# Logits, exponentials and slot products of the last pair in pieces, and row sums ahead of the second expert layer

## The chip, the cores and the metric

The kernel runs on one core of one Trainium2 chip. The metric is the device time of one execution in microseconds, as the median of several runs of a kernel.

## What is computed

Attention over keys and values that are averaged in groups of eight, and behind it a soft mixture of experts:

```python
k_p = k.reshape(B, H, Sp, pool, D).mean(axis=3)        # B = H = 8, S = 576, D = 64, pool = 8, Sp = 72
v_p = v.reshape(B, H, Sp, pool, D).mean(axis=3)
attn = softmax(scale * q @ k_p.T)
x = (attn @ v_p).transpose(0, 2, 1, 3).reshape(4608, 512)
logits = x @ phi                                       # 32 slots: 8 experts x 4
slot_input = softmax(logits, axis=0).T @ x             # over the 4608 tokens
slot_out[e] = relu(slot_input[e] @ w1[e]) @ w2[e]      # w1: 512 x 1024, w2: 1024 x 512, for each expert
out = softmax(logits, axis=1) @ slot_out
```

## The kernel before

The batch is worked off in four pairs of batch elements. A pair's tokens stand in nine tiles of 128 (t = 0 to 8), its heads in two halves of four (qd = 0, 1). For each half, eight score units (`score_unit`: two matmuls into `sc`, one ScalarE exponential into `exa`) are interleaved with nine `u_tile`s. A `u_tile` multiplies `exa` by the pooled values into a PSUM tile `u_ps` (two buffers), takes the reciprocal of the softmax sum on VectorE (`rec`), and scales the tile into `xsa`, on VectorE in one instruction or, with `by_scalar`, on ScalarE in four. The pooled values carry 32 more columns per head, the values' share of the slot logits. So each row of `xsa` holds per head 64 output values and 32 logit shares; summed over the heads these are the logits.

`dispatch` turns a pair into its share of the slot input. It sums the logit shares over the heads (`lg`), takes one exponential for all nine tiles (`ee`, ScalarE), and adds nine slot products `ee.T @ x` in `G_ps` on TensorE. For the first three pairs the sum over heads is eight matmuls with the identity, spread into the next pair's work by `combine`. For the last pair, with `by_vector`, it is one VectorE reduction over all nine tiles. `add_up` adds the result to the other pairs' (`Gb` for the last).

Then, in program order: `Gb` is transposed (`si_ps`), `turn` transposes `ee` into `cT` (the unnormalized weights of the last softmax), `hidden` makes the experts' first layer (`h_ps`, four experts side by side in TensorE's columns), `turn_hidden` transposes it (`hT_ps`). `hz` and `z_ps` prepare a correction for the last 128-row block of the last expert. `second_layer` adds the second layer in `so_ps`, experts 0 to 3, then 4 and 5, then 6 and 7 in pieces. `row_sums` sums `cT` over the slots with one-hot weights (`R_ps`), copies the sums to SBUF on ScalarE, transposes them (`RT_ps`) and takes their reciprocals. `busy(512)` is a dummy product of fp32 operands into `idle_ps`. At the end `begin` and `tiles` multiply tokens by slot outputs, scale them on ScalarE and VectorE in turn, and store them.

Up to the hidden layer a scheduler sets the order of TensorE, ScalarE and VectorE from the program; GpSimd keeps the written order throughout, and all engines do from `hidden` on. GpSimd issues all weight loads: w1 into `w1_sb` (named `w_sb` in the profile), w2 of experts 0 to 3 into the `big` buffers, 4 and 5 into `qTa`, 6 and 7 into `xsa`, the last in eight pieces by halves of the columns (L492), which wait until the slot products have read what they overwrite.

Of the kernel before, what the change touches and what calls it, by code (L numbers as in the profile page):

```python
# [18 lines left out]
def kernel(  # L19
# [66 lines left out]

    CUT6 = FJ - 5
    HC = DM // 2  # L90
    halves = [slice(0, HC), slice(HC, DM)]
    PIECES = ((E - 2, CUT6, FJ), (E - 1, 0, 4), (E - 1, 4, FJ - 1), (E - 1, FJ - 1, FJ))
# [215 lines left out]
        nc.scalar.activation(out=dst.rearrange("p r (i t) -> p r i t", t=NU),  # L308
                             in_=ps[:, :, 0:S // 2].rearrange("p r (t i) -> p r i t", i=NI), func=AF.Exp, scale=scale)

    def u_tile(pair, qd, t, ex, by_scalar=False):

        ps = ps_u.tile([128, HQ, XW + 1], FP, name="u_ps", tag="u")
        for hh in range(HQ):
            for b in range(2):
                if t < 8 and b != t // 4:
                    continue
                c = (t % 4 if t < 8 else 4) * 128
                rows = slice(0, 128) if t < 8 else slice(b * 64, (b + 1) * 64)
                nc.tensor.matmul(out=ps[rows, hh],  # L320
                                 lhsT=ex[b][:, hh].rearrange("p r t -> p (r t)")[:, c:c + rows.stop - rows.start],
                                 rhs=vp[(2 * pair + b) % 5][:, qd * HQ + hh, 0:XW + 1],
                                 start=True, stop=True)
        rec = small.tile([128, HQ], FP, name="rec", bufs=3)
        nc.vector.reciprocal(out=rec, in_=ps[:, :, XW])  # L325
        dst = xs[pair][:, t, qd * HQ:(qd + 1) * HQ, :]
        if by_scalar:
            for hh in range(HQ):
                nc.scalar.activation(out=dst[:, hh], in_=ps[:, hh, 0:XW], func=AF.Copy, scale=rec[:, hh:hh + 1])
        else:  # L330
            nc.vector.tensor_tensor(out=dst, in0=ps[:, :, 0:XW],  # L331
                                    in1=rec.rearrange("p h -> p h ()").to_broadcast([128, HQ, XW]), op=ALU.mult)

    def dispatch(x, ps, ee, by_vector=False):

        if by_vector:
            lg = small.tile([128, 9, NS], FP, name="lg", bufs=1)
            nc.vector.reduce_sum(out=lg, in_=x[:, :, :, D:XW].rearrange("p t h c -> p t c h"), axis=AX.X)  # L338
        else:
            lg = ps_m.tile([128, 9, NS], FP, name="lg_ps", tag="m")  # L340
            for h in range(H):
                nc.tensor.matmul(out=lg, lhsT=ident, rhs=x[:, :, h, D:XW], start=(h == 0), stop=(h == H - 1))
        nc.scalar.activation(out=ee, in_=lg.rearrange("p t s -> p t () s").to_broadcast([128, 9, NG, NS]), func=AF.Exp)  # L343
        yield
        for t in range(9):
            nc.tensor.matmul(out=ps, lhsT=ee[:, t].rearrange("p g s -> p (g s)"), rhs=x[:, t, :, 0:D],  # L346
                             start=(t == 0), stop=(t == 8))

# [22 lines left out]
    def combine(pair):  # L371

        ps = ps_m.tile([128, DM], FP, name="G_ps", tag="m")
        ee = small.tile([128, 9, NG, NS], BF, name="ee", bufs=1)
        parts = dispatch(xs[pair], ps, ee)
        next(parts)
        yield
        next(parts, None)
        add_up(pair, ps, G)
        yield  # L380
        for b in range(2):
            turn(pair, b, ee)
            yield
# [15 lines left out]
    for c, (n, t) in enumerate(quads + rest):  # L399
        for i in range(2 * t.shape[1]):  # L400
            place[n + i] = (i, c)

    def row_sums():

        ps = ps_m.tile([NC, 4, 128], FP, name="R_ps", tag="m")
        for c, (_, t) in enumerate(quads + rest):
            nc.tensor.matmul(out=ps[:, 0:2 * t.shape[1]].rearrange("p (s r) i -> p s r i", r=2),   # L407
                             lhsT=onehot[:, MAXC - 1 - c:MAXC - 1 - c + NC], rhs=t,
                             start=(c == 0), stop=(c == NC - 1), skip_group_check=True)
        sums = consts.tile([NC, 4, 128], FP)  # L410
        nc.scalar.copy(out=sums, in_=ps)
        ps = ps_m.tile([128, 4, NC], FP, name="RT_ps", tag="m")
        for i in range(4):
            nc.tensor.transpose(out=ps[:, i], in_=sums[:, i], identity=identf[0:NC, 0:NC])
        nc.vector.reciprocal(out=recR[:, 0:2], in_=ps[:, 0:2])
        nc.vector.reciprocal(out=recR[:, 2:4, 0:len(quads)], in_=ps[:, 2:4, 0:len(quads)])
# [21 lines left out]
    for pair in range(NP):  # L438
        for qd in range(2):
            if qd == 0:  # L440
                prep = chain(prepare_kq(pair + 1), prepare_v(pair + 1)) if pair + 1 < NP else None
                if pair == 0:
                    prep = chain(prepare_v(0), prep)
            ex = [exa[0:SP, (2 * pair + qd) % 2, b] for b in range(2)]
            for i in range(9):
                if i < 8:
                    score_unit(pair, i // 4 * H + qd * HQ + i % 4, ex[i // 4][:, i % 4])
                if i < 5:
                    if last is not None:
                        u_tile(*last[:2], 4 + i, last[2])  # L450
                else:
                    u_tile(pair, qd, i - 5, ex)
                step(prep)
                if pair == 0 and i % 2:
                    step(prep)
                if qd == 0 and pair > 0:
                    if i == 4:
                        comb = combine(pair - 1)
                        step(comb)
                    if i == 7:  # L460
                        step(comb)
                if qd == 1 and i in (2, 6):
                    step(comb)
            if qd == 1:
                for _ in prep or ():
                    pass
            last = (pair, qd, ex)
    load_w2(qTa, 4, 2)
    load_w2(xsa[:, 0:1], E - 2, 1, 0, CUT6)

    u_tile(*last[:2], 4, last[2], by_scalar=True)
    G_ps = ps_m.tile([128, DM], FP, name="G_ps", tag="m")
    ee = small.tile([128, 9, NG, NS], BF, name="ee", bufs=1)
    for i in range(1, 5):
        u_tile(*last[:2], 4 + i, last[2], by_scalar=i % 2 == 0)
    for _ in dispatch(xs[NP - 1], G_ps, ee, True):
        pass
    add_up(NP - 1, G_ps, Gb)
    def half_home(e, half):
        if e == E - 1:  # L480
# [66 lines left out]
    hidden(1)  # L547
    turn_hidden(0)
    turn_hidden(1)
    nc.vector.reduce_sum(out=recC, in_=C, axis=AX.X)  # L550
    nc.vector.reciprocal(out=recC, in_=recC)

# [15 lines left out]
    def busy(n):  # L568
        nc.tensor.matmul(out=idle[:, 0:n], lhsT=cTf[:, 0:128], rhs=cTf[:, 0:n], start=True, stop=True)
# [7 lines left out]
    so_a = post.tile([128, DM], BF)  # L577
    so = post.tile([128, DM], BF)

    out_a = exf.rearrange("p (n c) -> p n c", c=DM)  # L580
    out_b = w1f.rearrange("p (n c) -> p n c", c=DM)
    n = 0
    places = []
    for rows, base in GROUPS:
        home = out_a[:, n:n + rows] if n + rows <= 6 else out_b[:, n - 6:n - 6 + rows]
        places.append((home, out[base:base + 128 * rows].rearrange("(p r) c -> p r c", r=rows)))
        n += rows

# [42 lines left out]

    for e in range(4):
        second_layer(e)
    row_sums()
    busy(512)
    for e in range(4, E - 2):
        second_layer(e)
# [55 lines left out]
```

## Time and profile before

| | |
|---|---|
| median of 3 runs | 175.68 us (175.49 to 175.91) |
| profiled execution | span 179.6 us, the only time given for it |
| busy, of that span | PE 129.9, DVE 97.1, ACT 88.3, POOL 19.9 us |
| DMA | 41.13 MB moved, HBM read 61.93 MB, written 9.44 MB |
| mean granted TensorE clock | 0.892 |

Times in the rows are microseconds from the start of the span. PE is TensorE's matmuls, PEld its weight loads, DVE VectorE, ACT ScalarE, POOL GpSimd, SP the queue that issues the stores. L338 is line 338 of the kernel. In a timeline or group row stand the output and input tiles, their sizes, the count, and in brackets the idle time before and what ended it. In the chain of waits a row is start, length, engine, tile, line and count. In a table of windows each engine has its busy time and, in brackets, its instructions; the last three columns are the granted clock (1.00 is full), the share of the 16 DMA engines and GB/s. A matmul is counted with its drain, so the last of a group is longer than its share; a few matmul records can be missing.

### The profile page before, as it was taken

The page shows a single profiled execution, that of the slowest core. Times are in us where ns is not written, and L with a number is a line of the kernel's source. Part 1 is how long each engine was busy: PE and PEld are TensorE (multiplying, and loading weights), DVE is VectorE, ACT ScalarE, POOL GpSimd, SP SyncE. Part 2 cuts the span into 40 slices and gives each one's busy share as a digit, 9 for nine tenths or more (in the row PEclk, how much of TensorE's full clock was granted, in tenths as well). Part 3 has the DMA queues.
Part 4 walks back from the last instruction along what each step waited for, and adds up shares of the span by engine and source line. Part 5 has one row for each costly group of instructions (what it writes and reads, how often), then busy time and mean ns, then how long its engine had stood idle before and what let it go on. Part 6 is the DMA issues. An engine that isn't in the chain of part 4 may idle for free.

```text
span 179.6 us, 2853 instructions
## 1 busy us (share of the span) xinstructions
PE 129.9 (72%) x1106; PEld 70.2 (39%) x1106; DVE 97.1 (54%) x258; ACT 88.3 (49%) x168; POOL 19.9 (11%) x37
## 2 busy tenths in 40 slices
PE   0006888999899999999998996512996988798000
PEld 0002463565555655556555543300443232333000
DVE  5403353387868588785888629764335000599200
ACT  3201238986887649876599726232012012799100
POOL 7000111052100040000100004000700300000000
PEclk9999999999999999999999669655559999999755
DMA  5999999999999999999999999999999990699995
GB/s 197 242 209 233 207 220 216 213 224 203 204 220 216 216 207 220 225 204 219 208 230 204 221 217 210 228 206 223 214 210 207 196 181 7 225 342 428 480 394 235
DMA packets 10780, 41.13 MB, mean 229 GB/s; under 512 B 768, under 2 KB 6656, under 8 KB 7184
## 3 DMA queue, kind: packets, MB, share of 16 engines
q0 software_dynamic: 7440, 30.48, 83.9%
q1 hardware_dynamic: 3328, 10.49, 15.0%
q8 instruction: 8, 0.13, 0.3%
q14 instruction: 4, 0.03, 0.0%
HBM read 61.93 MB, written 9.44 MB: 397 GB/s over the span
## 4 chain that ended last, share of the span: by engine, by line
PE 51%; ACT 17%; DVE 14%; DMA 6%; issue 3%; POOL 1%; DVEq 0%; ACTq 0%; POOLq 0%
PE pool_ps L234 9%; ACT exa L308 7%; DMA phi_f<-in_moe_phi_dram 6%; PE G_ps L346 6%; PE sc L306 6%; PE u_ps L320 6%; PE q_ps L266 5%; DVE w_sb L575 4%; PE h_ps L521 3%; DVE xsa L331 3%; PE so_ps L542 3%; ACT vmeans L240 2%; DVE lg L338 2%; PE R_ps L407 2%; PE turn_ps L250 2%
## 5 line engine op out<-in xcount | busy, mean ns | idle before, releaser
L308 ACT ACTIVATE exa<-sc 72x576 bf16<-72x576 f32 x64 | 39.5, 652 | 5.1 <-PE sc L306 4.3
L331 DVE TENSOR_TENSOR xsa<-u_ps,rec 128x384 bf16<-128x384 f32 x69 | 37.4, 554 | 1.3
L320 PE MATMUL u_ps<-vp,exa 72*128 72x97 bf16 (+1 forms) x320 | 27.3, 217 | 4.5 <-DVE xsa L331 3.7
L320 PEld LDWEIGHTS <-exa 72*128 72x128 bf16 (+1 forms) x320 | 18.2, 104 | 16.0 <-DVE xsa L331 6.8
L306 PE MATMUL sc<-qTa,kp 64*72 64x288 bf16 x128 | 22.0, 309 | 1.9 <-ACT exa L308 1.5
L234 PE MATMUL pool_ps<-big,pmat 128*128 128x512 bf16 x64 | 18.6, 411 | 0.7 <-ACT qTa L270 0.6
L325 DVE RECIPROCAL rec<-u_ps 128x4 f32<-128x4 f32 x72 | 11.5, 172 | 12.8 <-PE u_ps L320 12.6
L346 PE MATMUL G_ps<-xsa,ee 128*128 128x512 bf16 x36 | 12.0, 496 | 6.6 <-ACT ee L343 6.6
L266 PE MATMUL q_ps<-ident,big 128*128 128x128 bf16 x144 | 12.5, 231 | 0.2
L186 PE MATMUL phi_ps<-spread,sel 128*128 128x256 bf16 x4 | 1.3, 397 | 15.1 <-DVE spread L181 15.1
L600 PE MATMUL f_ps<-so,cT 128*128 128x512 bf16 (+1 forms) x42 | 10.2, 337 | 1.8 <-ACT w_sb L573 0.8
L306 PEld LDWEIGHTS <-kp 64*72 64x72 bf16 x128 | 8.0, 108 | 8.3 <-issue 3.1
L575 DVE TENSOR_SCALAR w_sb<-f_ps,recR 128x512 f32<-128x512 f32 (+1 forms) x17 | 10.5, 683 | 0.4 <-PE f_ps L600 0.2
L266 PEld LDWEIGHTS <-big 128*128 128x128 bf16 x144 | 9.6, 104 | 2.4 <-issue 0.7
L242 DVE TENSOR_REDUCE rsum<-rest_ps 128x64 f32<-128x512 f32 x8 | 5.5, 692 | 9.3 <-PE rest_ps L238 9.2
L270 ACT COPY qTa<-q_ps 128x768 bf16<-128x768 bf16 x8 | 6.3, 794 | 7.8 <-PE q_ps L266 7.8
L272 DVE COPY qTa<-q_ps 128x768 bf16<-128x768 bf16 x16 | 8.8, 553 | 2.1 <-PE q_ps L266 2.0
L573 ACT ACTIVATE w_sb<-f_ps,recR 128x512 f32<-128x512 f32 (+1 forms) x17 | 9.6, 638 | 0.5 <-PE f_ps L600 0.3
L492 POOL DMA_DIRECT2D xsa<-in_moe_w_dram x8 | 6.0, 754 | 26.2 <-PE G_ps L346 15.3
L346 PEld LDWEIGHTS <-ee 128*128 128x128 bf16 x36 | 4.1, 120 | 12.3 <-ACT ee L343 6.8
L234 PEld LDWEIGHTS <-pmat 128*128 128x128 bf16 x64 | 5.8, 103 | 6.4 <-issue 2.3
L240 ACT CAST vmeans<-pool_ps 128x1024 bf16<-128x1024 f32 x4 | 4.0, 1012 | 6.8 <-PE pool_ps L234 6.8
(104 smaller groups left out, 155.1 us busy)
## 6 DMA issues: line engine op xcount, KB each, us to landing
w_sb<-in_moe_w_dram POOLq DMA_DIRECT2D x2, 3072.0 KB, 37.2
big<-in_q_dram POOLq DMA_DIRECT2D x4, 1152.0 KB, 12.0
big<-in_v_dram POOLq DMA_DIRECT2D x4, 1152.0 KB, 15.8
big<-in_moe_w_dram POOLq DMA_DIRECT2D x1, 4096.0 KB, 40.0
big<-in_k_dram POOLq DMA_DIRECT2D x3, 1152.0 KB, 21.4
out_dram<-w_sb SPq DMA_DIRECT2D x1, 3072.0 KB, 10.8
qTa<-in_moe_w_dram POOLq DMA_DIRECT2D x1, 2048.0 KB, 30.4
out_dram<-w_sb SPq DMA_DIRECT2D x1, 2048.0 KB, 7.5
```

The lines of the kernel that those rows point to most:

```text
L234: nc.tensor.matmul(out=ps, lhsT=pmat, rhs=src[:, t:full * POOL:POOL, :], start=(t == 0), stop=(t == POOL - 1))
L266: nc.tensor.transpose(out=ps[:, t].rearrange("p n i -> p (n i)"), in_=q_sb[pair][:, tt:tt + 2, :].rearrange("p t d -> p (t d)"), identity= ...
L272: nc.vector.tensor_copy(out=dst, in_=ps)
L306: nc.tensor.matmul(out=ps[:, r, 0:S // 2], lhsT=kp[pair][rows, n], rhs=qT[pair][rows, n].rearrange("p t i -> p (t i)"), start=True, stop=True)
L308: nc.scalar.activation(out=dst.rearrange("p r (i t) -> p r i t", t=NU), in_=ps[:, :, 0:S // 2].rearrange("p r (t i) -> p r i t", i=NI), fu ...
L320: nc.tensor.matmul(out=ps[rows, hh], lhsT=ex[b][:, hh].rearrange("p r t -> p (r t)")[:, c:c + rows.stop - rows.start], rhs=vp[(2 * pair + ...
L325: nc.vector.reciprocal(out=rec, in_=ps[:, :, XW])
L331: nc.vector.tensor_tensor(out=dst, in0=ps[:, :, 0:XW], in1=rec.rearrange("p h -> p h ()").to_broadcast([128, HQ, XW]), op=ALU.mult)
L346: nc.tensor.matmul(out=ps, lhsT=ee[:, t].rearrange("p g s -> p (g s)"), rhs=x[:, t, :, 0:D], start=(t == 0), stop=(t == 8))
L573: nc.scalar.activation(out=dst, in_=src, func=AF.Copy, scale=by)
L575: nc.vector.tensor_scalar(out=dst, in0=src, scalar1=by, scalar2=None, op0=ALU.mult)
L600: nc.tensor.matmul(out=ps, lhsT=tokens(n), rhs=so[:, cols], start=True, stop=True)
```

## The change

`dispatch` is split into `weigh` (logits by eight matmuls with the identity, then the exponential, for a range of tiles) and `gather` (the slot products of a range). The other pairs call both for all nine tiles. The last pair calls them for tiles 0 to 3, 4 to 6 and 7 to 8 in turn, and has no VectorE reduction. Tiles 6, 7 and 8 of its second half get places in the two `sc` buffers. ScalarE scales tiles 1, 3, 5 and 7 of that half, where it had 4, 6 and 8. `row_sums` moves from behind the second layer of experts 0 to 3 to behind `turn_hidden`; its second part, the transposes and reciprocals, stays where it was, as `turn_sums`. Four `busy(512)` follow it, where one did. Two constants are written otherwise with the same value.

```diff
-    CUT6 = FJ - 5
+    CUT6 = 3
...
-    def u_tile(pair, qd, t, ex, by_scalar=False):
-        ps = ps_u.tile([128, HQ, XW + 1], FP, name="u_ps", tag="u")
+    def u_tile(pair, qd, t, ex, by_scalar=False, ps=None):
+        if ps is None:
+            ps = ps_u.tile([128, HQ, XW + 1], FP, name="u_ps", tag="u")
...
-    def dispatch(x, ps, ee, by_vector=False):
-        if by_vector:
-            lg = small.tile([128, 9, NS], FP, name="lg", bufs=1)
-            nc.vector.reduce_sum(out=lg, in_=x[:, :, :, D:XW].rearrange("p t h c -> p t c h"), axis=AX.X)
-        else:
-            lg = ps_m.tile([128, 9, NS], FP, name="lg_ps", tag="m")
-            for h in range(H):
-                nc.tensor.matmul(out=lg, lhsT=ident, rhs=x[:, :, h, D:XW], start=(h == 0), stop=(h == H - 1))
-        nc.scalar.activation(out=ee, in_=lg.rearrange("p t s -> p t () s").to_broadcast([128, 9, NG, NS]), func=AF.Exp)
-        yield
-        for t in range(9):
+    def weigh(x, ee, t0, t1):
+        lg = ps_m.tile([128, t1 - t0, NS], FP, name="lg_ps", tag="m")
+        for h in range(H):
+            nc.tensor.matmul(out=lg, lhsT=ident, rhs=x[:, t0:t1, h, D:XW], start=(h == 0), stop=(h == H - 1))
+        nc.scalar.activation(out=ee[:, t0:t1], in_=lg.rearrange("p t s -> p t () s").to_broadcast([128, t1 - t0, NG, NS]),
+                             func=AF.Exp)
+
+    def gather(x, ps, ee, t0, t1):
+        for t in range(t0, t1):
             nc.tensor.matmul(out=ps, lhsT=ee[:, t].rearrange("p g s -> p (g s)"), rhs=x[:, t, :, 0:D],
                              start=(t == 0), stop=(t == 8))
...
-                    u_tile(pair, qd, i - 5, ex)
+                    u_tile(pair, qd, i - 5, ex, by_scalar=pair == NP - 1 and qd == 1 and i in (6, 8))
...
-    u_tile(*last[:2], 4, last[2], by_scalar=True)
+    x = xs[NP - 1]
     G_ps = ps_m.tile([128, DM], FP, name="G_ps", tag="m")
     ee = small.tile([128, 9, NG, NS], BF, name="ee", bufs=1)
-    for i in range(1, 5):
-        u_tile(*last[:2], 4 + i, last[2], by_scalar=i % 2 == 0)
-    for _ in dispatch(xs[NP - 1], G_ps, ee, True):
-        pass
+    wide = [ps_sc.tile([128, 2, 512], FP, name="sc") for _ in range(2)]
+    spare = [wide[i // 2][:, i % 2, 0:HQ * (XW + 1)].rearrange("p (h c) -> p h c", h=HQ) for i in range(3)]
+    for i in range(5):
+        u_tile(*last[:2], 4 + i, last[2], by_scalar=i % 2 == 1, ps=spare[i - 2] if i >= 2 else None)
+        if i == 2:
+            weigh(x, ee, 0, 4)
+    gather(x, G_ps, ee, 0, 4)
+    weigh(x, ee, 4, 7)
+    gather(x, G_ps, ee, 4, 7)
+    weigh(x, ee, 7, 9)
+    gather(x, G_ps, ee, 7, 9)
     add_up(NP - 1, G_ps, Gb)
...
     turn_hidden(1)
+    row_sums()
...
+    IN_A = 6
...
     for e in range(4):
         second_layer(e)
-    row_sums()
+    turn_sums()
+    busy(512)
+    busy(512)
+    busy(512)
     busy(512)
```

ScalarE before, from the last score exponential to the copies behind the hidden layer. `xsa` rows are quarter tiles, `ee` the exponential of the logits:

```order
L308 ACTIVATE exa<-sc 72x576
L329 ACTIVATE xsa<-u_ps,rec 128x96 x12
L343 ACTIVATE ee<-lg 128x1152
L526 ACTIVATE h_sb_1719<-h_ps 128x512
L526 ACTIVATE h_sb_1720<-h_ps 128x512
L562 CAST zT<-z_ps 128x256
L411 COPY sums<-R_ps 10x512
```

The same place now; `xsa<-sc` is a tile that was multiplied into one of the two `sc` buffers:

```order
L308 ACTIVATE exa<-sc 72x576
L330 ACTIVATE xsa<-u_ps,rec 128x96 x8
L340 ACTIVATE ee<-lg_ps 128x512
L330 ACTIVATE xsa<-u_ps,rec 128x96 x4
L330 ACTIVATE xsa<-sc,rec 128x96 x4
L340 ACTIVATE ee<-lg_ps 128x384
L340 ACTIVATE ee<-lg_ps 128x256
L536 ACTIVATE h_sb_1749<-h_ps 128x512
L536 ACTIVATE h_sb_1750<-h_ps 128x512
L411 COPY sums<-R_ps 10x512
L573 CAST zT<-z_ps 128x256
```

Three tiles by ScalarE have become four, the first exponential stands between the second and the third of them, and the copy of the row sums now stands ahead of `zT`.

TensorE before, behind the last `u_tile`:

```order
L320 MATMUL u_ps<-vp_103,exa 64x97
L346 LDWEIGHTS ee
L346 MATMUL G_ps<-xsa,ee 128x512
...
L361 LDWEIGHTS ee
L361 MATMUL c_ps<-ident,ee 128x128
```

and now, from the last logit matmul of the first piece (`sc` is tile 7):

```order
L339 MATMUL lg_ps<-xsa,ident 128x128
L346 LDWEIGHTS ee
L346 MATMUL G_ps<-xsa,ee 128x512
...
L321 MATMUL sc<-vp_103,exa 128x97
...
L346 MATMUL G_ps<-xsa,ee 128x512
L339 LDWEIGHTS ident
L339 MATMUL lg_ps<-xsa,ident 128x96
...
L339 MATMUL lg_ps<-xsa,ident 128x64
L346 LDWEIGHTS ee
L346 MATMUL G_ps<-xsa,ee 128x512
L361 LDWEIGHTS ee
L361 MATMUL c_ps<-ident,ee 128x128
```

The nine slot products stood together; now two stand ahead of tile 7, two behind it, three behind the second piece's logits and two behind the third's.

TensorE before, between the hidden layer's transposes and the second layer:

```order
L533 MATMUL hT_ps<-ident,h_sb_1720 128x128
L560 LDWEIGHTS hz
L560 MATMUL z_ps<-cT,hz 128x256
L542 LDWEIGHTS hT
L542 MATMUL so_ps<-big,hT 32x512
```

and now:

```order
L543 MATMUL hT_ps<-ident,h_sb_1750 128x128
L408 LDWEIGHTS onehot
L408 MATMUL R_ps<-cT,onehot 10x512
...
L408 MATMUL R_ps<-cT,onehot 10x256
L571 LDWEIGHTS hz
L571 MATMUL z_ps<-cT,hz 128x256
L552 LDWEIGHTS hT
L552 MATMUL so_ps<-big,hT 32x512
```

The ten products of `R_ps` stand ahead of `z_ps`; behind the second layer of experts 0 to 3 only the transposes `RT_ps` are left, with four dummy products after them.

More of the change, by code (lines that the diff above doesn't have):

```diff
@@ L374, in combine @@
         ee = small.tile([128, 9, NG, NS], BF, name="ee", bufs=1)
-        parts = dispatch(xs[pair], ps, ee)
-        next(parts)
+        weigh(xs[pair], ee, 0, 9)
         yield
-        next(parts, None)
+        gather(xs[pair], ps, ee, 0, 9)
         add_up(pair, ps, G)
@@ L401 @@
             place[n + i] = (i, c)
+    sums = consts.tile([NC, 4, 128], FP)
     def row_sums():
@@ L409, in row_sums, with turn_sums @@
                              start=(c == 0), stop=(c == NC - 1), skip_group_check=True)
-        sums = consts.tile([NC, 4, 128], FP)
         nc.scalar.copy(out=sums, in_=ps)
+    def turn_sums():
         ps = ps_m.tile([128, 4, NC], FP, name="RT_ps", tag="m")
@@ L584 @@
     for rows, base in GROUPS:
-        home = out_a[:, n:n + rows] if n + rows <= 6 else out_b[:, n - 6:n - 6 + rows]
+        home = out_a[:, n:n + rows] if n + rows <= IN_A else out_b[:, n - IN_A:n - IN_A + rows]
         places.append((home, out[base:base + 128 * rows].rearrange("(p r) c -> p r c", r=rows)))
```

## The prediction

> **What bounds the kernel now.** I read the windows of 1 us first, to see whether the memory or the engines set the end.
>
> ```profile
> 147.00:148.00 1.00, 1.00 (x17) 0.42 (x10) 0.00 (x0) 0.00 (x0) 0.00 (x0) 1.00 1.11 147
> 148.00:149.00 1.00, 1.00 (x5) 0.10 (x3) 0.00 (x0) 0.00 (x0) 0.00 (x0) 1.00 0.33 44
> 149.00:150.00 1.00, 1.00 (x11) 0.41 (x8) 0.00 (x0) 0.00 (x0) 0.00 (x0) 1.00 0.00 0
> ...
> 153.00:154.00 1.00, 0.86 (x13) 0.46 (x12) 0.96 (x3) 0.86 (x3) 0.00 (x0) 1.00 0.60 199
> ```
>
> The last three columns are the granted clock, the DMA share and GB/s. The loads run dry between 148 and 149 us, and the first result is stored from 153: for four microseconds memory waits for the engines. So the serial chain up to the first store sets the end; stores and final scaling follow it as a block. The chain that ended last, from the last token tiles to the second layer (start, length, what):
>
> ```profile
> 60.79 1.95 PE G_ps L346 x9
> ...
> 114.59 1.04 ACT xsa L329 x4
> ...
> 119.29 4.00 DVE lg L338
> 123.31 1.17 ACT ee L343
> 124.53 4.03 PE G_ps L346 x9
> 128.59 0.69 DVE Gb L353
> ...
> 130.33 5.32 PE h_ps L521 x58
> ...
> 136.33 0.73 PE hT_ps L533 x8
> ...
> 138.14 0.34 DVE hz L557
> 138.53 0.28 PE z_ps L560
> 138.81 1.84 PE so_ps L542 x32
> 140.65 3.99 PE R_ps L407 x10
> 144.66 0.58 ACT sums L411
> 145.29 0.41 PE RT_ps L414 x4
> 145.70 1.05 PE idle_ps L569 x2
> 146.76 0.98 PE so_ps L542 x16
> ...
> 151.07 0.48 ACT so_a L573
> ...
> 153.84 0.43 PE so_ps L542 x9
> ```
>
> Three steps (logits 4.00, exponentials 1.17, slot products 4.03 us) run strictly one after the other from 119.29 to 128.59. TensorE also idles 1.47 us from 137.06 (the end of hT_ps) to z_ps, and 0.65 us from the end of R_ps to RT_ps. The first row is the same slot product for another pair: 1.95 us, half of 4.03. The clock explains that:
>
> ```profile
> 99.00:100.00 1.00, 0.61 (x9) 0.43 (x6) 0.93 (x4) 0.81 (x2) 0.00 (x0) 0.83 0.98 205
> 106.00:107.00 1.00, 1.00 (x9) 0.49 (x8) 0.04 (x1) 0.00 (x0) 0.00 (x0) 0.76 1.25 262
> 113.00:114.00 1.00, 0.57 (x7) 0.38 (x8) 0.93 (x5) 0.00 (x0) 0.00 (x0) 0.66 0.74 156
> 133.00:134.00 1.00, 1.00 (x20) 0.39 (x12) 0.00 (x0) 0.03 (x1) 0.00 (x0) 0.60 0.78 164
> ```
>
> A granted clock between 0.50 and 1.00 dates the flip inside its row: down at 99.66, up at 106.48, down at 113.32, up at 133.80. Everything between 113.3 and 133.8, the stage that is edited, runs at half clock.
>
> **The change: the last tiles and the slot sums.** The last nine tiles (0 to 8 of the pair's second half) feed the logits. Prices:
>
> ```profile
> 109.95 0.65 ACT L308 ACTIVATE exa<-sc 72x576 bf16<-72x576 f32 x1
> 110.42 0.37 PE L320 MATMUL u_ps<-vp,exa 72*64 72x97 bf16 x8 [0.47 <-DVE xsa L331]
> 111.86 0.56 DVE L331 TENSOR_TENSOR xsa<-u_ps,rec 128x384 bf16<-128x384 f32 x1
> 113.22 0.56 DVE L331 TENSOR_TENSOR xsa<-u_ps,rec 128x384 bf16<-128x384 f32 x1
> 115.68 0.81 PE L320 MATMUL u_ps<-vp,exa 72*128 72x97 bf16 x8 [0.65 <-ACT xsa L329]
> 100.27 1.14 PE L342 MATMUL lg_ps<-xsa,ident 128*128 128x288 bf16 x4
> 133.97 0.60 ACT L526 ACTIVATE h_sb<-h_ps 128x512 bf16<-128x512 f32 x1 [9.49 <-PE h_ps L521]
> ```
>
> VectorE needs 0.68 us a tile (two pitches from 111.86 to 113.22), of which some 0.12 are the reciprocal that it keeps for ScalarE's tiles too; ScalarE needs 1.04 us. ScalarE now takes tiles 1, 3, 5 and 7 (before 4, 6, 8). Three tiles have PSUM places of their own, so tiles 6 and 8 are multiplied early; their last weights come from the exponential that ends at 110.60, and they stand before tile 8 of the first half (110.42 before), which holds that one to about 110.75 and VectorE by some 0.2 us: tile 0 ends at 112.64 instead of 112.42.
>
> From there, with 0.05 us a hand-over and four products at half clock 0.45: ScalarE has tile 1 from 112.8 to 113.8 and tile 3 from 114.6 to 115.65 (its PSUM buffer and reciprocal come from tile 1); VectorE does 2 and 4 between, and tile 5 is multiplied by 116.0. The logit matmuls: a piece of four tiles has 128 columns, so 0.13 us each at half clock (1.14/4 x 128/288). Seven of the first piece's eight lie beside other work, the last at 116.1. Exponentials: 0.60 us for 512 elements as in the L526 row, and along the line from there to the 1.17 for 1152 in the chain 0.49 for 384 and 0.37 for 256. So the first ends at 116.75; then ScalarE's tile 5 until 117.8, and tile 7 (behind two slot products on TensorE) from 118.4 to 119.45. TensorE's second logits 118.9 to 120.0, exponential to 120.55, three slot products (0.43 each) to 121.9, third logits to 123.0, exponential to 123.4, two slot products with their drain to 124.5. The slot sum starts at 124.55 where it started at 128.59: **4.0 us earlier**. Of the nine slot products seven lie in waits; only two follow the last exponential.
>
> Bounds: unseen are the hand-overs between the three engines, some ten on this path. At 0.03 to 0.10 us each the gain is 3.5 to 4.2; with the logits pieces at full clock 4.6.
>
> [...]
>
> **The change: row sums ahead.** R_ps starts right after hT_ps and covers the 1.47 us wait for hz; the ScalarE copy of 0.58 and the wait of 0.65 now lie beside so_ps (1.84). zT is queued behind that copy, but is first read after four more blocks. Against that, three more dummy products of 1.05 us stand before the second layer's fifth expert: 3.15 - 1.47 - 0.65 = **+1.0 us**. The rest of the constant edits (CUT6 = 3, IN_A = 6) give the same values and cost nothing.
>
> **The hidden layer.** h_ps took 5.32 us: half clock until 133.80, 3.5 us after its start at 130.3, then full. If the clock opens as long after its new start (126.3), the length stays; I allow 0.1.
>
> **Loads.** None may become late now. Their issue rows and times to landing:
>
> ```profile
> 108.39 0.70 POOL L120 DMA_DIRECT2D qTa<-in_moe_w_dram  x1 [18.57 <-ACT cT L366]
> qTa<-in_moe_w_dram POOLq DMA_DIRECT2D x1, 2048.0 KB, 30.4
> ...
> 125.86 2.99 POOL L492 DMA_DIRECT2D xsa<-in_moe_w_dram  x4 [15.35 <-PE G_ps L346]
> xsa<-in_moe_w_dram POOLq DMA_DIRECT2D x1, 64.0 KB, 17.6
> ```
>
> The fifth expert's weights land at 138.8 and would be read at 146.76 - 3 = 143.8. The last first-half piece (64 KB, third of the four issues from 125.86) lands by about 145.5; it is read about when so_a is scaled, at 151.07 and now near 148. The second halves are down by 149 (the dry window above) and are read from 153.84, now near 151. About 2 us of cover is left; beyond a shift of 5 us the loads would end the gain. The pieces' issues on GpSimd come earlier with the slot products, but wait behind the same full queue.
>
> **Sum.** -4.0 + 0.1 + 1.0 = -2.9 us, from 176.7 against the span of 179.6. The median of the runs is 175.68, 3.9 below that span (no other time is given for the profiled execution); I take the difference over unchanged: **172.8 us**. A difference under 0.35 us (0.2%) a measurement could not tell from no change.
>
> **Rivals.**
> *The clock opens no earlier (24%).* The four flips lie 6.82, 6.84 and 20.48 (3 x 6.83) us apart. If they keep to that grid, and it is tied to the kernel's start, the next after 126.97 is again 133.80, and the h products run at half clock throughout: 16 groups of four side by side, each as long as a slot product (4.03/9 = 0.43 with the drain left out), 6.9 us. 1.5 us are lost, total 174.3. Against: 3.5 us of dense h products sufficed before. [...]
>
> *The clock opens early (9%).* With slot products and logits spread from 117 on, the flip could come at 126.97. h_ps would then take 3.5 + 0.4 us, 1.5 less: 171.3. Against: on the path above TensorE waits a third of the time from 117 to 124, and the clock closed at 99.66 and 113.32 in rows where it was 0.61 and 0.57 busy.
>
> *Slower: the clock falls again in the moved block (7%).* R_ps uses ten columns of the array and now follows h at once. If it counted as idleness, the clock would halve near 137 to 140, before the dummies: four of them at twice 1.05 cost 4.2 us more, so +1.3, total 177.0. It decides where the granted clock is under 1 between 137 and 143. Against: R_ps ran 3.99 us alone before, and the rows from 147 stand at 1.00.
>
> *The pieces do not pay (8%).* Each of ten hand-overs takes 0.3 us more than counted, or TensorE, which works in order, holds tiles 5 and 7 behind a waiting logit matmul: 3 us, no gain, 175.7, a little either way. For it speaks that three engines now take turns where before each finished its step; against it, that the steps beside each other are short.
>
> **How the numbers follow.** The forecast holds 52%; its own range, from the gain of 3.5 to 4.6, is 172.2 to 173.3. Faster: 52 + 24 + 9 = 85%. The last rival splits into 5% no change and 3% slower; with the clock's fall 10% slower. The range goes from the early clock (171.3) to the late one with the smaller gain (174.3 + 0.5), 171.3 to 174.8, which leaves out the two last rivals, nearly whole, and what lies past either end of the others, some 2 in 10.
>
> **What would show it.** In the new profile the slot sum Gb should start at 124.5 (128.59 before), no long lg step stand on VectorE, ScalarE show three ee steps of about 0.60, 0.50 and 0.40, h_ps start near 126.3, z_ps follow R_ps without a gap, the fifth expert's so_ps start near 143.8, and the DMA gap before the stores shrink from 4 to about 1 us. I am wrong if Gb starts after 126, if h_ps takes over 6 us, or if the clock falls between h_ps and the fifth expert.

## The result, and the profile after

The changed kernel takes 177.25 us, the median of 4 runs (177.14 to 178.25). Against the kernel before the ratio is 1.0096, 95% interval 1.0066 to 1.0125: about 1.7 us slower, where I forecast 2.9 us faster. The before profile that the prediction argues from was an execution of about 181 us (its span of 179.6 and the 1.8 us that other executions take beyond theirs), 5 to 6 us longer than those whose median is 175.68, so below I compare with a new profile of the same kernel (span 173.9 us, time 175.69). Ratios here and below leave out executions more than 1.5% above the fastest of their kernel, which 33 of 116 of the kernel before were (all but one 178.3 to 181.5 us, at a mean clock of 0.891 to 0.917, the others at 0.901 to 0.927); the one that the prediction reads took as long.

The timeline of the changed kernel, at the steps that the prediction named (start, length, engine, line, operation, count, idle time before and what ended it):

```profile
112.37 0.60 ACT L340 ACTIVATE ee<-lg_ps 128x512 bf16<-128x512 f32 x1 [0.63 <-PE lg_ps L339]
115.92 0.49 ACT L340 ACTIVATE ee<-lg_ps 128x384 bf16<-128x384 f32 x1 [0.17 <-PE lg_ps L339]
118.26 0.38 ACT L340 ACTIVATE ee<-lg_ps 128x256 bf16<-128x256 f32 x1 [1.85 <-PE lg_ps L339]
119.34 0.67 DVE L353 TENSOR_TENSOR Gb<-G,G_ps 32x512 bf16<-32x512 f32 x1 [4.00 <-PE G_ps L346]
120.88 3.64 PE L531 MATMUL h_ps<-w_sb,siT 128*32 128x512 bf16 x64
138.78 1.90 PE L552 MATMUL so_ps<-qTa,hT 128*32 128x512 bf16 x16 [2.74 <-DMA qTa<-in_moe_w_dram]
149.36 0.47 ACT L584 ACTIVATE so_a<-so_ps,recC 128x256 bf16<-128x256 f32 x1 [0.21 <-PE so_ps L552]
154.43 7.33 DVE L586 TENSOR_SCALAR w_sb<-f_ps,recR 128x512 f32<-128x512 f32 x11
```

The same steps in the new profile of the kernel before:

```profile
115.11 4.00 DVE L338 TENSOR_REDUCE lg<-xsa 128x288 f32<-128x2304 bf16 x1 [1.11 <-ACT xsa L329]
119.15 1.16 ACT L343 ACTIVATE ee<-lg 128x1152 bf16<-128x1152 f32 x1 [4.06 <-DVE lg L338]
124.42 0.68 DVE L353 TENSOR_TENSOR Gb<-G,G_ps 32x512 bf16<-32x512 f32 x1 [5.31 <-PE G_ps L346]
125.96 3.64 PE L521 MATMUL h_ps<-w_sb,siT 128*32 128x512 bf16 x64
140.67 1.05 PE L542 MATMUL so_ps<-qTa,hT 128*32 128x512 bf16 x16
149.28 0.48 ACT L573 ACTIVATE so_a<-so_ps,recC 128x256 bf16<-128x256 f32 x1 [0.18 <-PE so_ps L542]
154.36 7.33 DVE L575 TENSOR_SCALAR w_sb<-f_ps,recR 128x512 f32<-128x512 f32 x11
```

The pieces do what they should: `Gb` starts 5.1 us earlier, h_ps is as long in both. The lead is 1.9 us at the fifth expert's products, where TensorE now waits 2.74 us for their weights, and nothing at the second half of `so_a`. The chain of waits names the holder. In the changed kernel it has two long transfers behind 104 us:

```profile
104.41 34.33 DMA qTa<-in_moe_w_dram
139.30 9.68 DMA xsa<-in_moe_w_dram
```

In the new profile of the kernel before, engines lead up to the second of them and no further:

```profile
134.63 3.99 PE R_ps L407 x10
138.64 0.57 ACT sums L411
139.22 9.69 DMA xsa<-in_moe_w_dram
```

The step there from `sums` to the transfer need not be a wait for `sums`: the fifth expert's weights land at 138.7 in both kernels, and the transfer starts some 0.55 us later in both. The last weights land at 148.9 and 149.0, and in the kernel before too TensorE waits for them a moment:

```profile
148.95 0.29 PE L542 MATMUL so_ps<-xsa,hT 128*32 128x256 bf16 x3 [0.36 <-DMA xsa<-in_moe_w_dram]
```

Chain and loads met there in the kernel before already; a shorter chain only waits longer.

So far the change is worth nothing. The loss stands behind 149, where the engines of both kernels do the same work at the same times (the last VectorE group starts 0.07 us apart and is 7.33 us long in both). Windows of 2 us, the last two columns the DMA share and GB/s; the changed kernel:

```profile
150.00:152.00 2.00, 1.54 (x11) 0.91 (x11) 1.16 (x3) 1.52 (x4) 0.00 (x0) 1.00 1.04 350
152.00:154.00 2.00, 1.92 (x10) 0.85 (x9) 1.88 (x5) 2.00 (x5) 0.00 (x0) 1.00 0.85 280
154.00:156.00 2.00, 1.80 (x7) 0.63 (x6) 2.00 (x4) 2.00 (x5) 0.00 (x0) 1.00 0.46 153
```

and the kernel before:

```profile
150.00:152.00 2.00, 1.54 (x11) 0.98 (x11) 1.24 (x3) 1.59 (x4) 0.00 (x0) 1.00 1.04 350
152.00:154.00 2.00, 1.91 (x10) 0.84 (x8) 1.88 (x5) 2.00 (x5) 0.00 (x0) 1.00 0.91 304
154.00:156.00 2.00, 1.80 (x8) 0.59 (x6) 2.00 (x4) 2.00 (x5) 0.00 (x0) 1.00 1.02 347
```

Row by row the engines agree; from 154 to 156 the DMA engines of the changed kernel move less than half. The DMA parts of the two pages (queue: packets, MB, share; then stores: count, KB each, us to landing) show what else ran. The changed kernel:

```profile
q8 instruction: 9, 0.15, 0.3%
...
out_dram<-w_sb SPq DMA_DIRECT2D x1, 3072.0 KB, 12.1
...
out_dram<-w_sb SPq DMA_DIRECT2D x1, 2048.0 KB, 8.8
out_dram<-w_sb SPq DMA_DIRECT2D x1, 1536.0 KB, 6.5
```

The kernel before:

```profile
q8 instruction: 8, 0.13, 0.3%
...
out_dram<-w_sb SPq DMA_DIRECT2D x1, 3072.0 KB, 10.8
...
out_dram<-w_sb SPq DMA_DIRECT2D x1, 2048.0 KB, 7.5
out_dram<-w_sb SPq DMA_DIRECT2D x1, 1536.0 KB, 5.2
```

Each of the three largest stores, all of them issued behind 153, lands 1.3 us later, and queue 8 carried one packet more. A packet is 16 KB (0.13 MB in 8). In the trace the ninth starts at 153.3 us and takes 1.41, shortly before the hole; the eight others fall among the loads in both kernels. Beside it the issue of the 512 KB store on the store queue takes 1.86 us, where it takes 0.57 in the kernel before:

```profile
153.24 1.86 SPq L603 DMA_DIRECT2D out_dram<-w_sb  x1
```

```profile
153.17 0.57 SPq L591 DMA_DIRECT2D out_dram<-w_sb  x1
```

### The profile page after: what moved, and what is told of

It reads as the page before. It is cut to its first block, busy times and chain, and to the rows that moved or that the text cites. A ratio compares the mean times of both kernels' runs of the same rounds, so it can differ in the third digit from the quotient of the medians.

```text
span 175.3 us, 2919 instructions
## 1 busy us (share of the span) xinstructions
PE 129.0 (74%) x1136; PEld 70.6 (40%) x1136; DVE 92.5 (53%) x256; ACT 89.2 (51%) x174; POOL 19.9 (11%) x37
## 4 chain that ended last, share of the span: by engine, by line
DMA 32%; PE 30%; ACT 12%; issue 11%; DVE 5%; POOL 1%; DVEq 0%; ACTq 0%; POOLq 0%
DMA qTa<-in_moe_w_dram 20%; PE pool_ps L234 9%; DMA phi_f<-in_moe_phi_dram 7%; DMA xsa<-in_moe_w_dram 6%; PE q_ps L266 5%; PE sc L306 4%; ACT exa L308 4%; DVE w_sb L586 4%; PE u_ps L321 4%; ACT kmeans L240 2%; ACT vmeans L240 2%; PE G_ps L346 2%; PE turn_ps L250 2%; PE lg_ps L339 1%; ACT qTa L270 1%
## 5 line engine op out<-in xcount | busy, mean ns | idle before, releaser
L332 DVE TENSOR_TENSOR xsa<-u_ps,rec 128x384 bf16<-128x384 f32 x66 | 35.8, 553 | 1.2
L321 PE MATMUL u_ps<-vp,exa 72*128 72x97 bf16 (+1 forms) x304 | 25.8, 214 | 2.0 <-DVE xsa L332 1.2
L306 PE MATMUL sc<-qTa,kp 64*72 64x288 bf16 x128 | 21.4, 302 | 1.8 <-ACT exa L308 1.3
L326 DVE RECIPROCAL rec<-u_ps 128x4 f32<-128x4 f32 x69 | 10.9, 172 | 12.2 <-PE u_ps L321 12.1
L266 PE MATMUL q_ps<-ident,big 128*128 128x128 bf16 x144 | 11.6, 219 | 0.8 <-DVE qTa L272 0.3
L346 PE MATMUL G_ps<-xsa,ee 128*128 128x512 bf16 x36 | 10.5, 427 | 1.8 <-ACT ee L340 1.7
L266 PEld LDWEIGHTS <-big 128*128 128x128 bf16 x144 | 8.7, 97 | 2.9 <-issue 1.3
L586 DVE TENSOR_SCALAR so<-so_ps,recC 128x256 bf16<-128x256 f32 x2 | 1.0, 484 | 14.7 <-PE so_ps L552 14.7
L584 ACT ACTIVATE so_a<-so_ps,recC 128x256 bf16<-128x256 f32 x2 | 0.9, 474 | 14.3 <-PE so_ps L552 14.3
## 6 DMA issues: line engine op xcount, KB each, us to landing
out_dram<-w_sb SPq DMA_DIRECT2D x1, 3072.0 KB, 12.1
```

What stands on the lines that cost most here:

```text
L266: nc.tensor.transpose(out=ps[:, t].rearrange("p n i -> p (n i)"), in_=q_sb[pair][:, tt:tt + 2, :].rearrange("p t d -> p (t d)"), identity= ...
L306: nc.tensor.matmul(out=ps[:, r, 0:S // 2], lhsT=kp[pair][rows, n], rhs=qT[pair][rows, n].rearrange("p t i -> p (t i)"), start=True, stop=True)
L321: nc.tensor.matmul(out=ps[rows, hh], lhsT=ex[b][:, hh].rearrange("p r t -> p (r t)")[:, c:c + rows.stop - rows.start], rhs=vp[(2 * pair + ...
L332: nc.vector.tensor_tensor(out=dst, in0=ps[:, :, 0:XW], in1=rec.rearrange("p h -> p h ()").to_broadcast([128, HQ, XW]), op=ALU.mult)
L584: nc.scalar.activation(out=dst, in_=src, func=AF.Copy, scale=by)
L586: nc.vector.tensor_scalar(out=dst, in0=src, scalar1=by, scalar2=None, op0=ALU.mult)
```

## The experiments

The letters in the expectations: theory A, the loads are the bound; B, TensorE's clock; C, the added dummy products and the moved sums; D, the ninth packet; A' is the earlier chain itself as the cause of the loss. Ratios are against the kernel before, run beside each.

**The kernel before, unchanged.**

> The kernel before, unchanged, for an execution that stands for its timed runs. The two profiles say that the change gained 4.3 us (span 179.6 to 175.3); the timed runs say that it lost 1.6 (175.7 to 177.2). Theory A (the loads were the bound already): the span is near 173.8; the chain in front is ahead of the profiled one by about 4 us up to the first h product, yet the last piece of the second-layer weights lands near 149, the second half of so_a starts at 149 to 149.5, and from there to the end it takes 24.5 us (after: 25.9). Theory B (TensorE's clock): the second half of so_a starts at 147 to 148, before the loads' end in the changed kernel (148.98), because the clock stands at 1.00 from 138 to 142, where it fell in the changed kernel. Either way the time is 175.7.

Span 173.9, the second half of `so_a` at 149.28, 24.6 us from there to the end (changed kernel: 25.9). Theory A holds on every number, and B does not: the clock is 1.00 from 138 to 142 here and 0.50 for part of that in the changed kernel, and both reach 149.3.

**The pieces alone.** The row sums in their old place, one dummy:

```diff
     turn_hidden(1)
-    row_sums()
...
+    row_sums()
     turn_sums()
-    busy(512)
-    busy(512)
-    busy(512)
     busy(512)
```

> The kernel before with the logits and slot products in pieces and ScalarE's new share, but the row sums in their old place with one dummy product behind them. Theory A, loads already the bound and the loss in the output stage: Gb at 119 to 120, but the second half of so_a still at 149; the half-0 stores start while loads run, and the time is that of the changed kernel, 176.8 to 177.4. Theory C (the loss is the three added dummies and the moved sums): 175.0 to 175.8, no loss. What I predicted on record would give 171.8.

Ratio 1.0101 (1.0053 to 1.0149), `Gb` at 119.38: the whole loss without the sums and the dummies. C is out as its cause.

No hole follows the ninth packet here, which starts at 156.1: the DMA share is 1.03 from 154 to 156 and 1.11 from 156 to 158, and the 512 KB store is issued in 0.57 us. Yet the 3 MB store lands in 12.2 us. The trace shows how, by the 128 packets of 24 KB in which it goes. In the kernel before, the last sixteen end together, from 172.04 to 172.22. Here fifteen do, from 172.01 to 172.18, and one ends at 173.54. In the 1.5 and 2 MB stores one in sixteen is 1.4 us late too.

**The sums and dummies alone.** The kernel before with `row_sums()` behind `turn_hidden(1)`, and `turn_sums()` and four `busy(512)` behind the fourth expert.

> The kernel before with only the row sums ahead of the second layer and four dummy products in place of one; logits and shares as before. Theory A: the second layer still waits for the loads, so 175.7, give or take 0.3. Theory C: all of the loss, 177.2. On record: +1.0, 176.7.

1.0041 (1.0011 to 1.0070), 8 packets. That is more than A allowed and less than C. The nine times compared fall in two groups, four from 175.59 to 176.42 and five from 176.97 to 177.31. The profile is of the fastest, with the second half of `so_a` at 149.16. With chain and loads ending together a longer chain has no cover, but how the slower five lose their time isn't shown.

**One dummy in the changed kernel** (three of the four `busy(512)` taken out).

> The changed kernel with one dummy product of 512 columns behind the row sums' transposes instead of four. Theory A: TensorE waits 3 us longer for the fifth expert's weights (5.9 us instead of 2.74), nothing else moves: 177.2. Theory B: the longer idle stretch keeps the clock down into the fifth expert's products, 178 or more. Theory C: the 3.15 us come back in part, 175.0 to 176.2.

1.0100 (1.0062 to 1.0137), 9 packets. The wait for the weights took up the 3 us:

```profile
138.70 1.90 PE L552 MATMUL so_ps<-qTa,hT 128*32 128x512 bf16 x16 [5.40 <-DMA qTa<-in_moe_w_dram]
```

TensorE stops 2.7 us sooner and starts again at the same time as in the changed kernel.

**Packets and instructions.** The changed kernel and the two others that lost 1%, with 2270 to 2282 records on TensorE (matmuls, weight loads, a few of its sequencer), had nine packets; the two with 2222 and 2234 had eight. The count of TensorE's records when each packet starts (before: the new profile):

```
before (2222 in all)       234  478  752 1000 1246 1528 1728 1995
changed (2282)             236  470  755 1000 1250 1525 1744 1981 2235
sums and dummies (2234)    236  496  746 1004 1250 1531 1728 2019
```

One packet for some 250 instructions: 16 KB each on the queue that the page calls instruction, and 250 to 255 records between two on average in these three, so I read them as TensorE's code. The change adds 24 identity matmuls and 3 dummies (two matmuls each), with a weight load for every one: 60 records, and it passes about 2235. The next runs add instructions and leave the rest as it is.

**Tiny products in front.** On zeros, ahead of TensorE's first input, in the kernel before:

```diff
+    tiny = ps_m.tile([128, 16], FP, name="tiny_ps", tag="m")
+    for _ in range(30):                      # 75, 150, 100 in the other runs
+        nc.tensor.matmul(out=tiny, lhsT=zeros[:, 0:128], rhs=zeros[:, 0:16], start=True, stop=True)
```

> The kernel before with 30 products of 16 columns on zeros at the very start, where TensorE waits for its first load until 15 us: 60 instructions more for TensorE, no work moved anywhere. The traces show a queue named q8 instruction with packets of 16384 bytes: 8 of them in the kernel before and with the sums alone moved, 9 in the changed kernel and in the two others that lost 1% (TensorE's records: 2222 and 2234 against 2270 to 2282). Theory D (each such packet, code for TensorE by its pace of one per some 250 instructions, keeps one DMA engine for about 1 us, and the kernel is bound by DMA from start to end): 9 packets, the ninth near 153 us from the start, the last store later by 1 to 1.5 us, 176.9 to 177.3. Theory A' (the loss comes of the earlier chain in front of the output stage): 8 or 9 packets, 175.7.

> As the one with 30, with 75 tiny products at the start (150 instructions): the ninth packet should come near 142, among the last loads instead of among the stores. Theory D: one DMA engine's work grows all the same, so the last piece of weights lands 0.5 to 1.4 us later (149.5 to 150.4) and the time is 176.5 to 177.2. If only a packet among the stores costs: 175.7. Theory A': 175.7.

> As before, with 150 tiny products at the start (300 instructions): ten packets. Theory D: two packets' price, 2 to 2.8 us, 177.7 to 178.5. Theory A': 175.7 to 176 (the products take under 9 us of TensorE before its first input lands).

With 30: nine packets, the ninth at 156.3, the three stores landing in 12.2, 8.9 and 6.6 us. The profile is of an execution of 179.62 us, but in the prediction's profile, which is longer still, they land in 10.8, 7.5 and 5.2. One of the six times is left by the rule for ratios, 176.93, at the lower end of D's range. With 75 the ninth packet comes among the loads, as the window from 145 to 148 shows:

```profile
q8 instruction: 1, 0.02, 2.0%
```

and the stores land in 10.8, 7.5 and 5.2 as before. Ratio 1.0024 (0.9997 to 1.0052): there it costs some 0.4 us, if anything, less than D gave it. With 150 there are ten, one at 141.9 and one at 162.1 (the profile is of an execution of 182.79 us): 1.0123 (1.0084 to 1.0162), 2.2 us from three times, inside D's range. The packet among the stores seems to be the dear one.

**One piece, few dummies.** The changed kernel with

```diff
-        if i == 2:
-            weigh(x, ee, 0, 4)
-    gather(x, G_ps, ee, 0, 4)
...
+    weigh(x, ee, 0, 9)
+    gather(x, G_ps, ee, 0, 9)
...
-        if n:
-            busy(n)
```

and one `busy(512)` of the four.

> The changed kernel with the last pair's logits by TensorE in one piece after all tiles, one dummy product of 512 columns behind the row sums' transposes, and without the two of 256 columns among the weight pieces: about 2230 records on TensorE, under the 2234 that still got on with 8 packets. The chain keeps about 2 us of its lead. Theory D: 8 packets, 175.4 to 175.9. Theory A': the loss stays, 176.8 to 177.3. My chain sum on record, if the loads did not bind: 173.7.

Eight packets, yet 1.0069 (1.0042 to 1.0096), so the time is not what D gave. The third column from the right, the granted clock, tells why the run settles nothing:

```profile
148.00:150.00 2.00, 2.00 (x16) 0.66 (x16) 0.98 (x3) 1.18 (x4) 0.00 (x0) 0.50 0.76 241
```

It was at half from 138 to 155, and the output products on `so_a` took 397 ns (median) in place of 271. I had removed two things at once, code and the dummies that stand around the load waits; whether the clock follows either of them is not shown.

**The whole late change with eight packets.** This kernel leaves out eight of the nine slot products and two of the eight heads' logits of each of the first three pairs, 60 instructions, and so computes something else; the last pair is the changed kernel's.

```diff
-        weigh(xs[pair], ee, 0, 9)
+        weigh(xs[pair], ee, 0, 9, H - 2)
         yield
-        gather(xs[pair], ps, ee, 0, 9)
+        nc.tensor.matmul(out=ps, lhsT=ee[:, 0].rearrange("p g s -> p (g s)"), rhs=xs[pair][:, 0, :, 0:D],
+                         start=True, stop=True)
```

> The changed kernel in all its parts, with work left out of the first three pairs: one slot product each instead of nine, logits over six heads instead of eight, 60 instructions less on TensorE (2222 records, as many as the kernel before). Everything from the last pair on is the changed kernel's. If the 1% is the ninth code packet among the stores: 8 packets, no hole in the stores, 175.4 to 175.9. If the changed chain itself costs it: 177.0 to 177.4. My sum on record: 172.8.

1.0027 (1.0000 to 1.0053), 8 packets, and the stores are the kernel before's again:

```profile
q8 instruction: 8, 0.13, 0.3%
...
out_dram<-w_sb SPq DMA_DIRECT2D x1, 3072.0 KB, 10.8
```

About two thirds of the 1% are gone with the packet. The runs lie from 175.43 to 177.25, those above 177 at a mean clock of 0.863, the others at 0.89 to 0.91, so what is left goes with the clock.

**The same by place.** The whole changed kernel with 75 and 100 tiny products in front; nothing is left out.

> The whole changed kernel with 75 products of 16 columns on zeros at the very start: 2432 records, nine code packets, the ninth at record 2240 and so near 138 us, among the loads, and none among the stores. If the place of the packet is what costs: 175.6 to 176.3, the time of the kernel before, with no hole in the stores. If the ninth packet costs wherever it falls, or the changed chain does: 177.0 to 177.4.

> As with 75, with 100 tiny products (2482 records): the ninth packet near 134, the tenth not reached (it would come at some 2494). The same: 175.6 to 176.3 if the place counts, 177.0 to 177.4 if the number does.

1.0041 (1.0013 to 1.0068) and 1.0016 (0.9983 to 1.0050). With 75 the median, 176.59, lies between the two ranges expected, and the one profile is of an execution of 367.66 us: nine packets, the last 29 us ahead of the first half of `so_a`, so it shows the order and no times. With 100 the window from 135 to 137.5 holds the ninth packet,

```profile
q8 instruction: 1, 0.02, 2.6%
```

and the stores land in 10.7, 7.4 and 5.1. (This execution took 177.27 us all the same, above the median of 176.15 of those compared: its clock was at half from 144.8 to 155.0.) The number of packets is the changed kernel's and so is the whole chain, and the time is about that of the kernel before. The place counts, and A', the chain itself, is out as the cause of the 1%.

**The wait filled.** 90 products of 16 columns behind the four `busy(512)`.

> The changed kernel with 90 products of 16 columns (2.6 us at 29 ns, the pace that they had at the start of the program) where TensorE waits 2.74 us for the fifth expert's weights. The ninth packet should come near 138, among the loads, and the clock stay open from 138 to 142. If a packet among the loads costs little (75 tiny products at the start: 0.4 us): 175.7 to 176.4. If every packet costs the same: 177.2.

1.0058 (1.0024 to 1.0092): a miss of the size. The packet moved to 145.0 and the stores landed in 10.8, but the group row of the fifth expert's products (count, min/median/max ns, first to last start)

```profile
L552 PE MATMUL so_ps<-qTa,hT x16: 379/379/390, 142.1 to 142.8; 128*32 128x512 bf16 x16
```

shows them at 142.1, where they started at 138.8 in the changed kernel. In that run the clock opened at 126.8, not 117.9: the chain was late, and little of the wait that I meant to fill was there.

**1 MB less to load.** In both kernels, with the last expert's first-layer weights left out (zeros in their place):

```diff
-            load_w1(5, 3)
+            load_w1(5, 2)
...
+    nc.vector.memset(w1_sb[:, E - 1], 0.0)
```

> The kernel before with 1 MB less to load: the last expert's first-layer weights are set to zero by VectorE at the start instead. 1 MB at the 213 GB/s of the loads is 4.9 us, so the last piece would land near 144. Theory A (chain and loads both end near 149 in the kernel before): the chain is the bound at once, the gain is what it waited, 0.4 to 0.8 us: 174.9 to 175.3. If the chain had more to spare: up to 4 us less.

> The changed kernel with the same 1 MB less to load. Theory A: the wait of 2.74 us for the fifth expert goes, the shortened chain sets the second half of so_a, near 146.5, and the time falls by 2.5 to 3 us to 174.3 to 174.8, of which 1.4 is still the ninth packet: below the kernel before with the same loads by 0.3 to 0.9 us. If the loads are not what holds the changed kernel: no more gain than the kernel before has, 176.5 to 177.

The kernel before: 0.9991 (0.9968 to 1.0014), less than the 0.4 to 0.8 us expected. The DMA engines stand empty for two microseconds (last columns), and yet the second half of `so_a` comes when it came with all loads. The windows:

```profile
142.00:144.00 2.00, 2.00 (x12) 0.68 (x9) 0.00 (x0) 0.00 (x0) 0.00 (x0) 1.00 0.78 103
144.00:146.00 2.00, 1.64 (x17) 0.63 (x16) 0.00 (x0) 0.47 (x1) 0.00 (x0) 1.00 0.00 0
```

while its timeline has

```profile
149.33 0.47 ACT L574 ACTIVATE so_a<-so_ps,recC 128x256 bf16<-128x256 f32 x1
```

The changed kernel: 0.9796 (0.9751 to 0.9840), from two of six times (172.22 and 172.69, under the 174.3 to 174.8 expected; the four that the rule for ratios leaves out are 175.77 to 179.43, so this gain rests on few executions). In the one of 172.69 TensorE has no wait for the fifth expert any more,

```profile
136.24 1.05 PE L553 MATMUL so_ps<-qTa,hT 128*32 128x512 bf16 x16
```

and the second half of `so_a` starts at 145.0, 4.3 us ahead of the kernel before with the same loads, though its ninth packet still falls among the stores, at 150.0 (12.1, 8.8, 6.5 us). So with shorter loads the change gains 3.4 us (172.45 against 175.85, the medians of the times compared), which has the sign of my chain sum. That the size is near its 2.9 is partly luck: the fifth expert's products start 4.8 us earlier than in the kernel before with the same loads (141.0), the last weights, at 144.6, still hold the second half of `so_a`, and the ninth packet costs as before. With the real loads the change gains nothing.

**Whole rows for the seventh expert.** An attempt to shorten the loads without leaving anything out: one transfer for its second-layer weights (`load_w2(xsa[:, 0:1], E - 2, 1)`), and no half pieces of it.

> The changed kernel with the seventh expert's second-layer weights loaded in one transfer, not three whole rows and two times five half rows. From 139 to 146, when half rows are under way, the loads move 195 GB/s at a DMA share of 1.44, before that 215 to 221. 0.66 MB of the 1.7 MB in half rows at the better rate is 0.3 us less; the half-0 stores start 1.6 us later, which should also fill the hole in the DMA share at 149 to 150 (0.66 to 0.82, some 0.4 us). If the loads bind the changed kernel: 0.3 to 0.8 us less than it, 176.4 to 176.9; the ninth packet stays among the stores. If the later half 0 costs more than that: 177.5 to 178.

> The kernel before with the same one transfer. Its chain and its loads both end near 149, so the shorter loads alone buy nothing and the first half's products wait for more: 175.7 to 177.

> The changed kernel with that one transfer and the 100 tiny products at the start, which put the ninth packet among the loads: 175.0 to 175.7, a little under the kernel before, if the loads bind; 176 to 176.5 if the later half 0 costs.

1.0178 (1.0131 to 1.0226), 1.0037 (1.0022 to 1.0052) and 1.0081 (1.0052 to 1.0110): worse in each (in the profile of the first the clock is at half from 138 to 148 as well). The hole that I meant to fill grew. In the kernel before, windows now read

```profile
148.00:150.00 2.00, 1.85 (x16) 0.91 (x16) 1.66 (x4) 1.70 (x5) 0.00 (x0) 1.00 0.66 199
150.00:152.00 2.00, 1.19 (x8) 0.54 (x7) 0.57 (x2) 1.50 (x4) 0.00 (x0) 1.00 0.74 243
```

where the DMA share was 0.89 and 1.04: the first half of `so_a` comes 1.3 us later (146.4 against 145.05), and with it the stores that should bridge the gap. No version here that computes the whole result beats the kernel before by more than can be measured.

## Why the prediction was wrong, step by step

- **The pieces** (-4.0). Right, and 1.1 us too small: `Gb` 124.42 to 119.34. The path itself was right: moved up by the 4.2 us between the two profiles of the kernel before, it has the first two exponentials at 112.0 and 115.9, and they start at 112.37 and 115.92. The 1.1 us are won behind 117.9, where the clock opened, earlier even than in my early rival; h_ps is unchanged at 3.64.
- **Sums and dummies** (+1.0). Right in kind, without effect: in the changed kernel three dummies less moved nothing but the wait for the fifth expert. In the kernel before they cost 0.4%, which stays unexplained.
- **Loads: "None may become late now."** This is the step that failed, and with it the reading that the chain up to the first store sets the end. I read 4 us of empty DMA and 2 us of cover from a profile with the second half of `so_a` at 155.03. In the executions that make up the median it starts at 149.28, a third of a microsecond behind the last weights, and the cover is nothing. The profiled execution had lost the time that the cover was made of: its clock fell at 99.66 for 6.8 us, inside the last scores, and opened again only at 133.80, against 124.24 in the new profile.
- **"I take the difference over unchanged."** The same error once more, and the sign of it was in the text: the span was 179.6, the median 175.68, which a launch overhead can't explain, since the span is the shorter of the two for one execution (173.9 and 175.69). Those 3.9 us and the 1.8 should have been taken off the chain first, and then nothing of the 4 us of empty DMA is left.
- **Not in the sum at all: TensorE's code.** I counted what the 24 logit matmuls take in time, not that they are instructions, which arrive in DMA packets of their own beside loads and stores (16 KB for some 250 of them here). The page showed 8 packets for 1106 matmuls and as many weight loads, so the next was near. Its price was 1.3 us at the stores, nearly all of the 1.4 us between the two spans (173.9 and 175.3).
- **Rivals.** That the pieces don't pay came nearest in time (175.7), by luck: the chain did shorten. The slower rival, a clock fall in the moved block, was seen (0.50 from 138.4 to 141.8, in the wait for the weights and not between R_ps and the dummies) and cost nothing, as the load came last anyway.

## What to carry to other kernels

Before spending a slack that a profile shows, compare the profiled execution's time with the median: if it is longer, find where it lost that time and take that off first. Where a chain and the loads end together, as at 149 us here, shortening one alone gained nothing (the chain 1.0016, with the ninth packet among the loads; the loads 0.9991) and both together 2% (0.9796, from two executions); leaving a transfer out in both kernels tells in one pair of runs which of them holds. Count a change's instructions as well as their time: the page's instruction queue showed 8 code packets before and 9 after, and the ninth, at 153.3 us, fell among the stores and cost 1.3 us.

## What the hardware showed that I had not expected

- A 16 KB code packet among the stores delayed the landing of those behind it: the 3 MB store landed in 10.7 to 11.0 us in the eleven profiles without one there and in 11.4 to 12.7 in the seven with one (the execution of 367.66 us is left out). With the packet among the loads instead, the same loads, the ratios were 1.0016 to 1.0058, the highest with a late chain (90 products in the wait). What the packet costs stands in the ends of the store's packets. In six of the seven the last one ends 0.8 to 1.8 us behind the median of the last sixteen, as if one of the 16 DMA engines had been held up and the store ended with it; without a packet among the stores it is 0.12 us at most. In the seventh, the changed kernel, it is 0.3; there the issue that took 1.3 us longer came first, and all packets behind it were later. The trace does not name the engine of a packet.
- The clock stood at half speed for 10.24 us (107.7 to 117.9) and for 3.41 us (138.4 to 141.8) in the changed kernel, with 20.48 us at full speed between the two. In the profile that the prediction reads, half speed lasted 6.83 and 20.48 us, with 6.83 us at full speed between. So the edges do not keep to the 6.83 us grid of my first rival: 10.24 and 3.41 us are one and a half of its steps and half of one.
